# Where the attention visits fire: kept apart, and barred in front of four of fourteen products, with two weight sums moved

## The chip, the cores and the metric

The kernel runs on one core of one Trainium2 chip. The metric is the device time of one execution in microseconds, as the median of several runs. A profiled execution gives the trace from which durations, waits and the chain of waits are read. "us" are microseconds.

## The reference

Two stages that follow one another: an attention whose softmax is replaced by a squared relu, for 8 batches of 12 heads with 448 tokens and head size 64, and a two-layer network with a squared relu on the 3584 resulting tokens.

```python
scores = scale * np.matmul(q, k.transpose(0, 1, 3, 2))
attn = np.maximum(scores, 0.0) ** 2 / S
x = np.matmul(attn, v)                # heads side by side: 3584 x 768
r = np.maximum(x @ w_in, 0.0)         # w_in 768 x 2048
out = (r * r) @ w_out                 # w_out 2048 x 768
```

Inputs and output are in fp32; the kernel computes in fp16 with fp32 sums in PSUM.

## The kernel before

**The work and its stages.** Attention is cut into 24 units (8 batches of 3; four heads a unit) of 7 tiles each, 168 tiles in all. A tile's way: `score` (L246) has TensorE write the scores to one of two PSUM slots (pool `s_p`, L71), then has ACT take their relu into an `at` tile (L258); a DVE multiplication squares it in place (`square`, L371). When the seven tiles of a unit are squared, `av_unit` (L303) runs 28 matmuls into a slot (L319), and ACT copies the result to `xt` (L325). Two tiles are scored per **visit** (`visit`, L373). A visit is named here by its first tile: visit 88 scores tiles 88 and 89. In a visit the first tile is scored, then an AV unit runs if the last tile of a unit was scored in an earlier visit, then the second tile is scored. A visit in which a unit begins also calls `prefetch` (L329): two DMA transposes on SP for the unit two further on, a load of its v and the loads of q and k for a later unit on POOL.

The network is computed for pairs of batches. For the first pair the hidden layer is computed directly (`h_group`, L414, 16 groups a batch). From batch 2 on it goes by a fast scheme with 7 instead of 8 block products (`h_period`, L471): each batch has two periods (`i0` 0 and 4), and each period two sets s of such products, 14 in all, numbered 0 to 13 in the order of the table `order` (L528). A product is six matmuls of 128x224. Some products start a fresh PSUM bank; others add into the bank that an earlier one left, once ACT has copied it (`copy`, L488) or DVE has added from it (`plus`, L493). In that table a row reads: set, block product, which bank of the set, fresh or not, what follows.

```python
(0, 1, 0, True, lambda: copy(0, 0, "m1", "a")),       # product 0
(1, 1, 0, True, lambda: copy(1, 0, "m1", "b")),       # product 1
(0, 6, 0, False, lambda: copy(0, 0, "u2", "c")),      # product 3
(1, 6, 0, False, lambda: copy(1, 0, "u2", "d")),      # product 4
(0, 5, 1, True, lambda: copy(0, 1, "m5", "a")),       # product 6
(0, 7, 0, False, lambda: plus(0, 0, "m5", True, True)),  # product 7
(1, 7, 0, False, lambda: copy(1, 0, "u3", "b")),      # product 8
(0, 4, 0, False, lambda: relu21(0)),                  # product 10
(1, 4, 0, False, lambda: relu21(1)),                  # product 11
```

The second layer (the w_out stage of each pair, `o_groups`, L608) takes pairs of 128-token rows through seven products of eight matmuls (128x384), in the order 1, 2, 6, 5, 7, 4, 3 of their names; the first product of the next pair of rows, or at the end of the stage products of the next h period, run between products 7 and 4 of the pair. Its sums of rows are DVE additions (`sums`, L596, L606), its results go out through ACT (L635, L683) and DVE (L640) to `osb` and by SP to DRAM.

**The order.** `steps` is one list of TensorE matmuls with a planned cost each: 0.1892 in h groups, 0.096 in h periods, 0.1625 in w_out. Their running sum is the planner's clock, which leaves the visits' own time out. `events` is a list of due times on that clock: visits, prefetches, DVE sums. The loop at the end (L906) walks the steps; in front of a step that is marked as an edge it fires all events whose time has come. In an h period the first matmul of every product is an edge (L565), in w_out the first matmul of every product (an edge of the kind 2, product 4, looks 1.6 ahead for one event). [...] the place at which an event fires decides behind which instructions of ACT and DVE its own stand.

The visits of a pair of batches are spread evenly (L861 to L864) from one bound to the next, 6.5 before the end of the first batch's h periods: due times are 2.19 apart while the attention of batches 2 and 3 is done (visits 42 to 82), 3.27 for batches 4 and 5, 2.83 for batches 6 and 7. Sums of x for a pair's first batch (`sums_x`, L453) are due in the last 6 units of the w_out stage before it. Six of the eight sums of w_in (`sums_w1`, L166, one DVE operation of 128x1536 each) fire in batch 1's h groups, two in the first w_out stage (L854); these two make w_in's last block, which block product 7 reads from batch 2 on.

Of the kernel before, what the change touches and what calls it, by code (L numbers as in the profile page):

```python
# [17 lines left out]
def kernel(  # L18
# [147 lines left out]
    def sums_w1(i):  # L166


        op, c = divmod(i, 2)
        now_ve(0.9)  # L170
        lo, hi = slice(0, NM // 2), slice(NM // 2, NM)
        a11, a12, a21, a22 = (w1[c][:, lo], w1[c][:, hi], w1[c + 2][:, lo],
                              w1[c + 2][:, hi])
        if op < 3:
            wsum[op, c] = late["ws"].tile(
                [P, NM // 2, 512], FP16, name=f"ws{op}{c}", tag=f"ws{op}{c}")
        if op == 0:
            nc.vector.tensor_add(wsum[0, c], a21, a22)
        elif op == 1:
            nc.vector.tensor_sub(wsum[1, c], wsum[0, c], a11)  # L180
        elif op == 2:
            nc.vector.tensor_sub(wsum[2, c], a12, wsum[1, c])
        else:
            nc.vector.tensor_sub(a21, a11, a21)
# [144 lines left out]
    def prefetch(m):  # L329
        if m >= NUN:  # L330
            return
        dma_transpose(m)
        if m > NPE:
            load_v(m)
        if m + 2 < NUN:
            load_qk(m + 2)
# [10 lines left out]
    def flush(rest=True):  # L347
        for d in (due, due_g) if rest else (due,):
            while d:
                put(d)  # L350
# [11 lines left out]
    def now_ve(cost, lag=0.25):  # L362
        at_ve[0] = max(at_ve[0], at_pe[0] + lag) + cost
# [5 lines left out]
    def square(at, lag=0.0):  # L369
        due.append((at_pe[0] + lag, 0.54,  # L370
                    lambda: nc.vector.tensor_mul(at, at, at), 0))  # L371

    def visit(tiles, turn=None, lag=2, most=3):  # L373
        now[0] += 1
        for t in tiles:
            if t % J == 0 and t >= NPE * J:
                prefetch(t // J + 2)
        if big:
            for t in tiles[:1]:
                score(t)  # L380
            av_unit()
            for t in tiles[1:]:
                score(t)
            at_pe[0] += 0.19 + 0.19 * len(tiles)
            for i, t in enumerate(tiles):
                square(ats[t], 0.6 + 0.85 * i)
            return
        for t in tiles:
            score(t, 2)
        if turn is not None:  # L390
            pe_transpose(turn)
        flush()
        av_some(lag, most)
        for t in tiles:
            square(ats[t])
        flush()
# [12 lines left out]
    def g_of(b):  # L409
        if b // 2 not in gts:  # L410
            gts[b // 2] = g_p.tile([P, NF, 2 * S], FP16, name="g", tag="g")
        return gts[b // 2]
# [58 lines left out]
    def h_period(b, i0, extra):  # L471

        z = (b % 2) * S
        XY = [[None, None], [None, None]]
        keep: dict = {}

        def gs(s, hi, right=None):
            f = i0 + 2 * s + (8 if hi else 0)
            c = (slice(z, z + S) if right is None
                 else slice(z + Q, z + S) if right else slice(z, z + Q))  # L480
            return g_of(b)[:, f:f + 2, c]

        def acc(s, y):
            return XY[s][y][:, 0:S].rearrange("p (r c) -> p r c", r=2)

        def copy(s, y, nm, tag):
            t = late["m"].tile([P, S], FP32, name=nm, tag=tag)
            nc.scalar.activation(out=t, in_=XY[s][y][:, 0:S], func=AF.Copy)  # L488
            keep[s, nm] = t.rearrange("p (r c) -> p r c", r=2)

        def plus(s, y, nm, hi, right):
            now_ve(0.54)
            nc.vector.tensor_add(gs(s, hi, right), acc(s, y), keep[s, nm])  # L493

        def rest(g, relu, lag):

            t = at_pe[0] + lag
            due_g.append((t, 0.32 if relu is g else 0.2, lambda: nc.vector.tensor_scalar(  # L498
                out=relu, in0=relu, scalar1=0.0, scalar2=None, op0=ALU.max), b))
            due_g.append((t, 0.54, lambda: nc.vector.tensor_mul(g, g, g), b))  # L500

        def relu21(s):
            nc.scalar.activation(out=gs(s, True, False), in_=acc(s, 0), func=AF.Relu)  # L503
            rest(gs(s, True), gs(s, True, True), 0.8)

        def c12(s):
            plus(s, 1, "u2", False, True)
            g = gs(s, False)
            rest(g, g, 0.0)

        def left(k, f, m):

            c, n = f // 4, slice((f % 4) * P, (f % 4 + 1) * P)
            if k in (1, 2):
                return w1[c][:, m + NH * (k - 1), n]
            if k in (4, 7):
                return w1[c + 2][:, m + (NH if k == 4 else 0), n]
            return wsum[{5: 0, 6: 1, 3: 2}[k], c][:, m, n]

        def right(k, m):  # L520
            if k in (1, 2):
                return xts[b][:, m + NH * (k - 1), 0:Q]
            if k in (3, 7):
                return xts[b][:, m + (NH if k == 3 else 0), Q:S]
            return xsum[b, {5: 0, 6: 1, 4: 3}[k]][:, m]


        order = (  # L528
            (0, 1, 0, True, lambda: copy(0, 0, "m1", "a")),
            (1, 1, 0, True, lambda: copy(1, 0, "m1", "b")),  # L530
            (0, 2, 1, True, lambda: plus(0, 1, "m1", False, False)),
            (0, 6, 0, False, lambda: copy(0, 0, "u2", "c")),
            (1, 6, 0, False, lambda: copy(1, 0, "u2", "d")),
            (1, 2, 1, True, lambda: plus(1, 1, "m1", False, False)),
            (0, 5, 1, True, lambda: copy(0, 1, "m5", "a")),
            (0, 7, 0, False, lambda: plus(0, 0, "m5", True, True)),
            (1, 7, 0, False, lambda: copy(1, 0, "u3", "b")),
            (1, 5, 1, True, lambda: plus(1, 1, "u3", True, True)),
            (0, 4, 0, False, lambda: relu21(0)),
            (1, 4, 0, False, lambda: relu21(1)),  # L540
            (0, 3, 1, False, lambda: c12(0)),
            (1, 3, 1, False, lambda: c12(1)))

        FREE = {2: 0.6, 5: 0.6, 7: 0.1, 9: 0.6, 12: 0.6, 13: 1.0, 16: 0.6}

        def step(p, r, m):
            s, k, y, fresh, end = order[p]

            def run():
                if fresh and r == 0 and m == 0 and k != 5:  # L550
                    XY[s][y] = mm_tile(s)
                nc.tensor.matmul(  # L552
                    XY[s][y][:, r * Q:(r + 1) * Q],
                    lhsT=left(k, i0 + 2 * s + r, m), rhs=right(k, m),
                    start=(fresh and r == 0 and m == 0), stop=(m == NH - 1),
                    skip_group_check=not (fresh and r == 0))
                if r == 1 and m == NH - 1:
                    end()
                    for fn in extra.get(p, ()):
                        fn()  # L560
                    nx = min(n for n in FREE if n > p)
                    fill(at_pe[0] + (nx - p) * 0.576 + 0.25 + FREE[nx])
            return run

        return [(0.096, step(p, r, m), r == 0 and m == 0)  # L565
                for p in range(14) for r in range(2) for m in range(NH)]

    def store(row, osb, c, eng, eng2=None):
# [258 lines left out]
    T_H = NF * T_G  # L827
# [4 lines left out]
    events = []  # L832
# [18 lines left out]
    for i in range(6):  # L851
        events.append((T_H + (8 + i) * T_G, lambda i=i: sums_w1(i)))
    for i in range(2):
        events.append((2 * T_H + 3 + 3 * i, lambda i=i: sums_w1(6 + i)))  # L854
    for m in (6, 7):
        events.append((T_H + (1 + 3 * (m - 6)) * T_G, lambda m=m: prefetch(m)))
    at0 = T_H + 8 * T_G
    for pr in range(1, B // 2):
        t0 = 2 * NB0 * pr
        end = begin[pr] + T_S - 6.5  # L860
        gap = (end - at0) / 21  # L861
        for i in range(21):
            ts = [t0 + 2 * i, t0 + 2 * i + 1]
            events.append((at0 + i * gap, lambda ts=ts: visit(ts)))  # L864
        at0 = end
        for i in range(4):
            events.append((begin[pr] - 6 + i, lambda b=2 * pr, i=i: sums_x(b, i)))
    events.append((at0 + 0.3, lambda: visit([])))

    def pre(pr, i):  # L870
        def run():
# [29 lines left out]
                steps += periods[b, i0]  # L901
        steps += outs[pr][0]

    clock = 0.0
    ev = deque(sorted(events, key=lambda e: e[0]))
    for cost, fn, edge in steps:  # L906
        fired = 0
        while ev and edge and ev[0][0] <= clock + (1.6 if edge == 2 and not fired else 1e-3):
            ev.popleft()[1]()
            fired += 1  # L910
        if fn is not None:
            at_pe[0] += cost
            fn()
        clock += cost
# [31 lines left out]
```

## Time and profile before

| | |
|---|---|
| Time, median of three runs | 377.74 us (377.57 to 377.84) |
| The profiled execution | 377.92 us, span 376.1 us |
| Granted TensorE clock | 0.999 |
| h periods of batches 2 and 3 | 123.75 to 167.1 us |
| w_out stage of the second pair, with the first products of batch 4 | 167.1 to 217.1 us |
| h periods of batches 4 and 5 | 217.1 to 260.5 us |
| w_out stage of the third pair | 260.5 to 297.7 us |

In lines of the profile, PE is TensorE's matmuls, PEld its weight loads, DVE VectorE, ACT ScalarE, POOL GpSimd, SPq the queue that issues DMAs on SyncE. A line of the timeline has the start, the time from the first start to the last end, engine, line and operation, "out<-in" with the names of the tiles, the shape, and how many instructions are merged in it. In brackets stands how long the engine had been idle and what ended that. The first of two overlapping records is not shortened, so the distance between starts says more than the lengths. L254 are scores, L319 AV units, L552 products of h periods, L733 products of w_out.

### The profile page before, as it was taken

Reading aid. Unit: us, or ns where it says so; the run is one execution under the profiler, and the core shown is the slowest. Engines: PE = TensorE matmul, PEld = TensorE weight load, DVE = VectorE, ACT = ScalarE, POOL = GpSimd, SP = SyncE. Lnnn points to the kernel's source line nnn. Section 1 sums busy time; section 2 is a strip of 40 time slices with the busy share of each in tenths; the row PEclk is TensorE's granted clock in tenths of the full one; section 3 lists DMA queues with packets and bytes.
Section 4 is the critical chain, followed back from the end, with each engine's and each line's share of the span. In section 5 each row is a group of like instructions: output and inputs, shape, how many; then the busy total and the mean of one; then the engine's idle time right before and its main releaser. Section 6 shows DMA issues by size and latency. Waiting matters only on the chain.

```text
span 376.1 us, 8798 instructions
## 1 busy us (share of the span) xinstructions
PE 363.3 (97%) x3600; PEld 231.1 (61%) x3600; DVE 280.4 (75%) x518; ACT 247.6 (66%) x370; POOL 107.2 (29%) x128
## 2 busy tenths in 40 slices
PE   7899999999999999999999999999999999999994
PEld 3554444454555778875555578877455588985663
DVE  1886677997767699797775758978966788995542
ACT  2997894786777797776665678887666785531220
POOL 8545431837432354413043144050000000000001
PEclk9999999999999999999999999999999999999999
DMA  8999999999999999959699999692232300002333
GB/s 115 199 204 205 204 204 149 132 140 129 203 138 175 157 129 122 91 81 75 115 117 129 195 153 86 83 103 53 49 86 65 83 23 2 2 0 65 95 95 84
DMA packets 121159, 42.64 MB, mean 113 GB/s; under 512 B 100832, under 2 KB 117760, under 8 KB 121120
## 3 DMA queue, kind: packets, MB, share of 16 engines
q0 software_dynamic: 82912, 23.01, 62.6%
q1 hardware_dynamic: 38048, 18.98, 26.4%
q8 instruction: 28, 0.46, 0.5%
q10 hardware_dynamic: 160, 0.10, 0.1%
q14 instruction: 11, 0.09, 0.1%
HBM read 45.61 MB, written 11.01 MB: 151 GB/s over the span
## 4 chain that ended last, share of the span: by engine, by line
PE 80%; DVE 9%; ACT 6%; issue 2%; DMA 1%; POOLq 0%; POOL 0%; ACTq 0%; DVEq 0%
PE mm L733 31%; PE mm L552 22%; PE mm L422 9%; PE slot L254 9%; PE slot L319 7%; ACT at L258 5%; DVE at L371 3%; DVE g L493 1%; DVE g L500 1%; DMA q<-in_q_dram 1%; DVE s L606 1%; PE slot L225 1%; DVE osb L640 1%; DVE g L498 1%; ACT m L488 1%
## 5 line engine op out<-in xcount | busy, mean ns | idle before, releaser
L258 ACT ACTIVATE at<-slot 128x896 f16<-128x896 f32 x168 | 146.0, 920 | 32.6 <-PE slot L254 32.5
L371 DVE TENSOR_TENSOR at<-at 128x896 f16<-128x896 f16 x168 | 99.9, 618 | 19.3 <-ACT at L258 18.8
L108 POOL DMA_DIRECT2D qs<-in_q_dram x36 | 35.5, 987 | 117.7 <-DMA qT<-qs 110.0
L733 PEld LDWEIGHTS <-s 128*128 128x128 f16 x440 | 41.6, 98 | 32.4 <-issue 3.9
L254 PE MATMUL slot<-qT,kT 64*64 64x448 f16 x756 | 57.9, 360 | 2.3 <-ACT at L258 1.6
L552 PEld LDWEIGHTS <-w 128*128 128x128 f16 x576 | 54.4, 98 | 5.9 <-issue 5.4
L552 PE MATMUL mm<-xt,w 128*128 128x224 f16 x432 | 48.6, 259 | 0.0
L733 PEld LDWEIGHTS <-g 128*128 128x128 f16 x336 | 31.5, 98 | 24.0 <-issue 5.0
L552 PEld LDWEIGHTS <-ws 128*128 128x128 f16 x432 | 40.2, 98 | 6.7 <-issue 6.7
L733 PE MATMUL mm<-b,g 128*128 128x384 f16 x224 | 40.7, 326 | 0.0
L733 PE MATMUL mm<-b,s 128*128 128x384 f16 x216 | 39.6, 326 | 0.3 <-DVE s L606 0.2
L422 PE MATMUL mm<-xt,w 128*128 128x448 f16 x192 | 39.8, 354 | 0.0
L733 PE MATMUL mm<-t,s 128*128 128x384 f16 x224 | 39.5, 326 | 0.0
L254 PEld LDWEIGHTS <-kT 64*64 64x64 f16 x756 | 19.9, 104 | 30.4 <-issue 25.5
L108 POOL DMA_DIRECT2D ks<-in_k_dram x36 | 35.0, 975 | 11.5 <-DMA b<-in_moe_w_out_dram 5.8
L640 DVE SCALAR_TENSOR_TENSOR osb<-mm,u 128x384 f32<-128x384 f32 (+1 forms) x30 | 16.2, 542 | 27.0 <-ACT u L635 19.3
L635 ACT ACTIVATE u<-mm 128x384 f32<-128x384 f32 x28 | 13.7, 491 | 33.2 <-PE mm L733 31.8
L573 POOL DMA_DIRECT2D out_dram<-osb x2 | 1.1, 564 | 120.7 <-DVE osb L640 120.7
L552 PE MATMUL mm<-x,ws 128*128 128x224 f16 x288 | 34.4, 259 | 0.9 <-ACT m L488 0.9
L319 PE MATMUL slot<-at,vt 64*64 64x448 f16 x588 | 32.2, 350 | 0.8 <-DVE at L371 0.7
L500 DVE TENSOR_TENSOR g<-g 128x896 f16<-128x896 f16 x48 | 29.7, 619 | 1.1 <-ACT g L503 0.2
L493 DVE TENSOR_TENSOR g<-mm,m 128x448 f16<-128x448 f32 x36 | 22.0, 619 | 9.4 <-ACT m L488 4.1
(69 smaller groups left out, 395.6 us busy)
## 6 DMA issues: line engine op xcount, KB each, us to landing
out_dram<-osb SPq DMA_DIRECT2D x52, 192.0 KB, 3.3
vt<-in_v_dram POOLq DMA_DIRECT2D x24, 224.0 KB, 6.9
qs<-in_q_dram POOLq DMA_DIRECT2D x36, 112.0 KB, 5.3
ks<-in_k_dram POOLq DMA_DIRECT2D x36, 112.0 KB, 5.6
w<-in_moe_w_in_dram POOLq DMA_DIRECT2D x8, 384.0 KB, 11.7
b<-in_moe_w_out_dram POOLq DMA_DIRECT2D x4, 768.0 KB, 17.1
q<-in_q_dram POOLq DMA_DIRECT2D x6, 224.0 KB, 8.1
k<-in_k_dram POOLq DMA_DIRECT2D x6, 224.0 KB, 8.5
```

Of the source, the lines that this page charges most:

```text
L108: nc.gpsimd.dma_start(out=t[:, :, hh, :], in_=heads(src, n)[:, hh].rearrange("p (j d) -> p j d", d=D))
L254: nc.tensor.matmul(ps[c, hh, 0:S], lhsT=kT[r, j, c], rhs=qT[r, :, c], start=True, stop=True)
L258: nc.scalar.activation(out=at, in_=ps[:, :, 0:S], func=AF.Relu, scale=SK)
L319: nc.tensor.matmul(ps[64 * hh:64 * hh + 64, hp, 0:S], lhsT=vt[r, hh, j * D:(j + 1) * D], rhs=at[r, hh, :], start=(j == 0), stop=(j == J - 1))
L371: lambda: nc.vector.tensor_mul(at, at, at), 0))
L422: nc.tensor.matmul(cell[0][:, 0:S], lhsT=w1[f // 4][:, m, (f % 4) * P:(f % 4 + 1) * P], rhs=xts[b][:, m, :], start=(m == 0), stop=(m == NM ...
L493: nc.vector.tensor_add(gs(s, hi, right), acc(s, y), keep[s, nm])
L500: due_g.append((t, 0.54, lambda: nc.vector.tensor_mul(g, g, g), b))
L552: nc.tensor.matmul(XY[s][y][:, r * Q:(r + 1) * Q], lhsT=left(k, i0 + 2 * s + r, m), rhs=right(k, m), start=(fresh and r == 0 and m == 0), ...
L635: nc.scalar.activation(out=t, in_=X[0][:, 0:HALF], func=AF.Copy, scale=CO)
L640: nc.vector.scalar_tensor_tensor(out=osb[row][:, c], in0=acc[0][:, 0:cc.stop - cc.start], scalar=CO, in1=keep[nm][:, cc], op0=ALU.mult, op ...
L733: nc.tensor.matmul(acc[0][:, 0:HALF], lhsT=left()[:, f], rhs=right[:, f], start=(fresh and f == 0), stop=(f == KH - 1), skip_group_check=n ...
```

## The change

- In an h period the first matmul of products 0, 1, 6 and 8 is no longer an edge: no event of any kind fires in front of them.
- Visits of batches 2 to 7 carry a third entry. Such an event fires only if the clock is at least 1.5 past the last one that fired; otherwise the loop stops there for this step, and the events behind it in the list wait as well.
- The two sums of w_in in the first w_out stage are due 6 and 14 after its begin, where they were due 3 and 6 after it.

```diff
-        return [(0.096, step(p, r, m), r == 0 and m == 0)
+        return [(0.096, step(p, r, m), r == 0 and m == 0 and p not in (0, 1, 6, 8))
                 for p in range(14) for r in range(2) for m in range(NH)]
...
-        events.append((2 * T_H + 3 + 3 * i, lambda i=i: sums_w1(6 + i)))
+        events.append((2 * T_H + 6 + 8 * i, lambda i=i: sums_w1(6 + i)))
...
-            events.append((at0 + i * gap, lambda ts=ts: visit(ts)))
+            events.append((at0 + i * gap, lambda ts=ts: visit(ts), True))
...
-    events.append((at0 + 0.3, lambda: visit([])))
+    events.append((at0 + 0.3, lambda: visit([]), True))
...
-    clock = 0.0
+    clock, last = 0.0, 0.0
...
         while ev and edge and ev[0][0] <= clock + (1.6 if edge == 2 and not fired else 1e-3):
+            if len(ev[0]) == 3:
+                if clock < last + 1.5:
+                    break
+                last = clock
             ev.popleft()[1]()
             fired += 1
```

## The prediction

> **What bounds the kernel now.** I read the page first (busy shares, chain of waits), then the timeline of TensorE over the h and w_out stages, then ACT's and DVE's timelines round each gap.
>
> ```profile
> PE 363.3 (97%) x3600; PEld 231.1 (61%) x3600; DVE 280.4 (75%) x518; ACT 247.6 (66%) x370; POOL 107.2 (29%) x128
> ...
> PE 80%; DVE 9%; ACT 6%; issue 2%; DMA 1%; POOLq 0%; POOL 0%; ACTq 0%; DVEq 0%
> ```
>
> TensorE carries 80% of the chain, ACT and DVE 15%: what can be won is where TensorE stands still for one of those two. A record of a matmul is longer than the distance to the next, so I measure by starts. In the h periods a product of six matmuls starts 0.576 us after the one before it; a visit of two tiles in between adds 0.60, and one that also holds an AV unit adds 1.92 (28 matmuls, 1.32). Whatever goes beyond that is a stall. TensorE in the first period of batch 3:
>
> ```profile
> 146.24 0.57 PE L254 MATMUL slot<-qT,kT 64*64 64x448 f16 x8
> 146.75 1.32 PE L552 MATMUL mm<-xt,w 128*128 128x224 f16 x12
> 147.91 0.74 PE L552 MATMUL mm<-x,ws 128*128 128x224 f16 x6
> 149.06 0.73 PE L552 MATMUL mm<-x,ws 128*128 128x224 f16 x6 [0.41 <-ACT m L488]
> ...
> 152.54 0.74 PE L552 MATMUL mm<-x,ws 128*128 128x224 f16 x6
> 153.61 1.31 PE L552 MATMUL mm<-x,w 128*128 128x224 f16 x12 [0.33 <-DVE g L493]
> ```
>
> 147.91 to 149.06 is 1.15 for a product of 0.576: a stall of 0.576. Product 4 adds into the bank that product 1 left, and must wait for ACT's copy of it. ACT at that time:
>
> ```profile
> 146.41 0.54 ACT L488 ACTIVATE m<-mm 128x448 f32<-128x448 f32 x1 [1.03 <-PE mm L552]
> 146.85 1.72 ACT L258 ACTIVATE at<-slot 128x896 f16<-128x896 f32 x2
> 148.44 0.56 ACT L488 ACTIVATE m<-mm 128x448 f32<-128x448 f32 x1
> ```
>
> The visit stood in front of product 1, so its two relus of scores (starts 0.80 apart) lie ahead of product 1's copy. At 153.61 the same goes by way of DVE: the visit in front of product 6 delays the copy of m5, the addition after product 7 waits for it, product 10 for the addition.
>
> The w_out stages have another sort of stall, between visits that stand close together:
>
> ```profile
> 90.76 0.56 DVE L640 SCALAR_TENSOR_TENSOR osb<-mm,u 128x384 f32<-128x384 f32 x1 [0.90 <-ACT u L635]
> 91.24 1.15 DVE L371 TENSOR_TENSOR at<-at 128x896 f16<-128x896 f16 x2
> 92.44 0.38 PE L319 MATMUL slot<-at,vt 64*64 64x448 f16 x4 [0.15 <-DVE at L371]
> ...
> 120.01 0.38 PE L254 MATMUL slot<-qT,kT 64*64 64x448 f16 x4 [0.26 <-ACT at L258]
> 120.82 0.38 PE L254 MATMUL slot<-qT,kT 64*64 64x448 f16 x4 [0.43 <-ACT at L258]
> ```
>
> First an AV unit waits for squares of tiles scored one product earlier; then scores wait for the two slots in PSUM. From 80 us to the end all stalls over 0.025 us sum to 6.75 us, the most that any order of this work could save there.
>
> [...] the copy starts at 148.44, 1.59 after the two relus ahead of it began. [...] here 97% busy hides those 6.75 us. [...] The trace has records of 0.92 and 0.55 and, back to back, starts 0.80 and 0.43 apart; I use the last.
>
> **The change, part by part.** An event fires at the first allowed step at which the planner's clock has reached its due time, so both orders can be worked out by hand from the step costs and due times. For the order before, each visit so placed shows up in the trace at its product.
>
> *Products 0, 1, 6 and 8 barred.* Removed, with the stall read at each: visit 88 (named by its first tile) from product 1 to 2 of batch 3 (149.06: 0.576); 90 from 6 to 7 (153.61: 0.492); 120 from 1 to 2 of batch 4 (219.19: 0.408); 122 from 6 to 7 (223.74: 0.492); 128 from 8 to 9 of its second period (235.92: 0.407); 136 from 0 to 2 in batch 5's second period (251.63: 0.407). These are all the stalls of over 0.1 us in the h periods but the 0.220 of the last AV unit, which stays. Sum **2.78**. Do the new places cost as much? In front of 2, the copies of products 0 and 1 are ahead of the relus; the next copy needed is product 3's, delayed to 2.05 after the visit's start and wanted by product 7 at 3.4. In front of 7, product 8's copy ends 2.6 after it and product 11 starts at 2.8. The trace has visits in front of 2 (124.42), 7 (303.18), 9 (142.19) and 12 (154.85) without a stall over 0.046. I take nothing.
>
> *Visits kept 1.5 apart.* On the planner's clock visits 54/56, 56/58, 60/62, 64/66 and 146/148 are 1.30 apart and 72/74 are 0.58. The second of each pair carries a stall: 1.024 (92.95), 0.109 (94.96), 0.114 (101.50), 0.110 (108.05), 0.552 (272.59) and 0.955 (121.14). They become 2.60 apart or, 72/74, 1.73, so the waiting work has at least 1.15 more, over any of these. Sum **2.86**.
>
> *What this pushes together.* Blocked visits hold back all events behind them. In the first w_out stage visits end up 2.60 apart and the surplus runs into batch 2: eight visits (72 to 86, in front of 2, 5, 9, 12 twice) where there were six. In that stretch:
>
> ```profile
> 123.75:134.98 11.23, 11.23 (x139) 8.60 (x138) 8.10 (x14) 9.54 (x15) 2.36 (x4) 1.00 1.24 167
> 134.98:145.58 10.60, 10.60 (x131) 9.06 (x130) 9.82 (x20) 9.18 (x15) 8.79 (x10) 1.00 1.61 136
> ```
>
> The columns after the length are PE, weight loads, DVE, ACT and POOL. ACT is busy 18.7 of 21.8 us; four more relus (3.2) make 21.9 of 23.0, as the two visits bring 1.2 us of TensorE work from elsewhere. DVE has 17.9; four more squares at 0.535 make 20.1. Both still fit, ACT barely. Walking ACT's queue through the two periods with these spacings, I find one wait: visit 78 holds an AV unit, its second score needs the slot of its first, whose relu then ends about 0.17 late. Bounds: nothing, or a stall of the kind above (mean 0.46) after four of the eight visits, 1.9. I take **0.4**: the 0.17 and half a stall.
>
> *The sums of w_in.* Two DVE additions of 0.95 move from 40.23 and 42.83 on the clock to 42.83 and 51.93; their results are first read by product 7 of batch 2's two periods, clock 67.7 and 75.7. Count and engine stay; nothing queued behind them on DVE is needed within 0.95. Zero. The sums of x for batch 2 are held back by at most 3.8; the last is read by product 10, 4.6 later. Zero.
>
> *DMAs moved along.* Every seventh tile's visit issues two transposes on SP and, on POOL, a load of v and four of q and k. They move up to 4.9 later, but what reads them is the visit seven further on, which moves too. The shortest distance, visit 70 to 84, is 15.3 of clock plus seven visits (4.2) and two AV units (2.6), about 22 us; transposes land 2.9 to 10.5 us after issue. On SP the order of stores and transposes stays as it is; POOL's waits are for its own buffers. Zero.
>
> Sum: 2.78 + 2.86 - 0.4 = **5.25**. The profiled execution has a span of 376.1, so 370.9 there; it was timed at 377.92, against a median of 377.74, so 377.74 - 5.25 = **372.5**.
>
> **Rivals.** *Crowding in batch 2 or 3 (17%).* The 1.9 above applies in place of 0.4: 374.0; with DVE's squares of g pushed into batch 3, where it was idle only some 2.3 of 21.5 us, up to 374.6. For it: ACT at 95%. Against: visits in front of 6, 10 and 13 at 128 to 134 us were as dense and cost nothing.
>
> *Only the h stalls go (10%).* DVE, not the spacing, holds the w_out stalls and they come back elsewhere: 377.74 - 2.78 + 0.4 = 375.4. For it: DVE is in the chain throughout 262 to 272. Against: spacing undoes the wait at 120.82 by construction.
>
> *Slower (4%).* Score slots in batch 2: with two slots and ACT behind, each of the eight visits waits as visit 74 did, 0.955 each, 7.6 in all: 377.74 - 5.25 + 7.6 = 380.1. It decides from the sixth visit that waits in full. Against: 1.73 of clock plus 0.6 is more than the 1.6 that two relus take.
>
> *It does nothing that can be told (3%)*: stalls are made good later, at the DVE-bound end of a stage: 377.7.
>
> **How the numbers follow.** My own case has 66%, from 371.8 (no cost at all, and some of the other 1.1 us of stalls gone too) to 373.5. Reaching to 374.6 takes in the crowding rival and leaves out the others, about 2 in 10. Runs of before lie within 0.27 us; 0.2% is 0.75 us, about what can be told from no change. Faster 0.93, same 0.03, slower 0.04.
>
> **What would show it.** Right: no PE wait on L488 or L493 in batches 3 to 5 over 0.1 us; the six w_out stalls gone; batch 2's two periods about 1.6 us longer (two visits and the 0.4). Wrong: new waits on "ACT m", "ACT u" or "ACT at" at 125 to 150 us beyond 1 us in all, or the DVE waits before L319 still there.

## The result: a quarter of the gain that was forecast

| | before | changed |
|---|---|---|
| Median, six runs each | 377.71 us (377.57 to 378.11) | 376.38 us (375.29 to 376.92) |
| Ratio to before, 95% interval | | 0.9959 (0.994 to 0.9978) |
| Span of the profiled execution | 376.1 us | 375.1 us |
| Granted TensorE clock there | 0.999 | 0.994 |
| All stalls from 80 us on, by starts (slowed matmuls included) | 6.75 us | 5.95 us |

The change makes the kernel faster by 1.3 us; 5.25 was forecast, in a range whose slow end was 374.6 us. The six runs of the changed kernel fall in two groups: three at 376.88 to 376.92 with a granted clock of 0.993 or 0.994 (the profiled one among them), three at 375.29 to 375.89 with 0.998 or 0.999. Why is part of the finding.

**The profile after.** The page's rows that were shown of before (line numbers behind L562 are two higher here):

```profile
PE 363.1 (97%) x3600; PEld 230.9 (62%) x3600; DVE 279.8 (75%) x518; ACT 247.7 (66%) x370; POOL 107.4 (29%) x128
...
PEclk9999999999999999999899999999999999999999
...
PE 83%; DVE 8%; ACT 4%; issue 2%; DMA 1%; POOL 0%; POOLq 0%; DVEq 0%; ACTq 0%
```

ACT and DVE have fallen from 15% to 12% of the chain. New is an 8 in the row of the clock, in the slice of 178 to 188 us.

The places that the prediction walked through look as forecast. TensorE and ACT in the first period of batch 3, where visit 88 had cost 0.576:

```profile
144.87 0.57 PE L254 MATMUL slot<-qT,kT 64*64 64x448 f16 x8
145.37 0.75 PE L552 MATMUL mm<-xt,w 128*128 128x224 f16 x6
145.96 1.31 PE L552 MATMUL mm<-x,ws 128*128 128x224 f16 x12
147.11 0.74 PE L552 MATMUL mm<-xt,w 128*128 128x224 f16 x6
```

```profile
144.46 1.06 ACT L488 ACTIVATE m<-mm 128x448 f32<-128x448 f32 x2 [0.23 <-PE mm L552]
145.42 1.72 ACT L258 ACTIVATE at<-slot 128x896 f16<-128x896 f32 x2
```

Both copies (144.46) now stand ahead of the two relus, and products 3 and 4 (145.96, twelve matmuls in one piece) run through. The AV unit of the first w_out stage, which had waited a microsecond for squares, starts at 91.30 right behind its scores:

```profile
91.09 0.38 PE L254 MATMUL slot<-qT,kT 64*64 64x448 f16 x4
91.30 1.49 PE L319 MATMUL slot<-at,vt 64*64 64x448 f16 x28
```

All twelve stalls that the prediction took off (5.65 us) are gone. What came in their place is in the second w_out stage:

```profile
177.74 0.57 PE L254 MATMUL slot<-qT,kT 64*64 64x448 f16 x8
178.24 1.47 PE L735 MATMUL mm<-b,g 128*128 128x384 f16 x8
181.87 4.29 PE L735 MATMUL mm<-t,s 128*128 128x384 f16 x16 [2.15 <-DVE s L608]
186.08 0.50 PE L254 MATMUL slot<-qT,kT 64*64 64x448 f16 x4
```

From 178.24 to 181.87 pass 3.63 us for eight matmuls of 0.163 each: a stall of 2.32, in which TensorE waits for the row sums of the second pair of row blocks. Then sixteen matmuls take 4.2 us where 2.6 are usual. The windows view of TensorE for 3.41 us of that (length, PE busy, clock, DMA share, GB/s) has the clock at half:

```profile
182.96:186.37 3.41, 3.41 (x15) 0.50 1.08 156
```

DVE's timeline shows what stands ahead of the row sums (174.69 is an output addition, L608 the row sums):

```profile
174.69 0.55 DVE L642 SCALAR_TENSOR_TENSOR osb<-mm,u 128x384 f32<-128x384 f32 x1
175.16 0.62 DVE L500 TENSOR_TENSOR g<-g 128x896 f16<-128x896 f16 x1
175.69 0.39 DVE L498 TENSOR_SCALAR g<-g 128x896 f16<-128x896 f16 x1
176.12 0.63 DVE L500 TENSOR_TENSOR g<-g 128x896 f16<-128x896 f16 x1
...
179.31 0.39 DVE L498 TENSOR_SCALAR g<-g 128x896 f16<-128x896 f16 x1
179.74 0.62 DVE L500 TENSOR_TENSOR g<-g 128x896 f16<-128x896 f16 x1
180.40 0.69 DVE L608 TENSOR_TENSOR s<-g 128x1024 f16<-128x1024 f16 x1
181.12 0.69 DVE L608 TENSOR_TENSOR s<-s,g 128x1024 f16<-128x1024 f16 x1
```

Eleven operations that finish g, the hidden activations (relu L498, square L500), stand there in a row, 5.2 us. They are work of batch 3's h periods. `rest` (L495) does not issue them but puts them into the queue `due_g`; `fill` (L357) issues them when the planner sees room on DVE; and before a second pair of row blocks is summed, `ahead` (L622) calls `flush_g(2 * B)`, which issues all that is left, since the sums read g. Of the eleven, `fill` issues the first two behind product 7 and `flush_g` the other nine. Before the change there were four, one by `fill` and three by `flush_g`:

```profile
177.82 0.55 DVE L640 SCALAR_TENSOR_TENSOR osb<-mm,u 128x384 f32<-128x384 f32 x1
178.29 0.38 DVE L498 TENSOR_SCALAR g<-g 128x896 f16<-128x896 f16 x1
178.70 0.63 DVE L500 TENSOR_TENSOR g<-g 128x896 f16<-128x896 f16 x1
179.24 0.39 DVE L498 TENSOR_SCALAR g<-g 128x896 f16<-128x896 f16 x1
179.66 0.63 DVE L500 TENSOR_TENSOR g<-g 128x896 f16<-128x896 f16 x1
180.32 0.69 DVE L606 TENSOR_TENSOR s<-g 128x1024 f16<-128x1024 f16 x1
181.05 0.69 DVE L606 TENSOR_TENSOR s<-s,g 128x1024 f16<-128x1024 f16 x1
```

The product that reads these sums started at 182.57 then, without a stall:

```profile
181.26 1.47 PE L733 MATMUL mm<-b,g 128*128 128x384 f16 x8
182.57 2.76 PE L733 MATMUL mm<-t,s 128*128 128x384 f16 x16
```

**The theory**, then: with the visits in their new places, two more of them in batch 2, more of g is left undone, the put-out in the second w_out stage grows from 4 to 11 operations, and the stall that this makes, 2.32 us, is what halves TensorE's clock in some runs (0.50 for 3.41 us in the profiled one). **Rivals**: the spacing of visits alone does it by crowding batch 2; the half clock comes by itself and has nothing to do with the stall; crowding itself, not the put-out, eats the gain.

### The profile page after: what moved, and what is told of

It reads as the page before. It is cut to its first block, busy times and chain, and to the rows that moved or that the text cites. A ratio compares the mean times of both kernels' runs of the same rounds, so it can differ in the third digit from the quotient of the medians.

```text
span 375.1 us, 8794 instructions
## 1 busy us (share of the span) xinstructions
PE 363.1 (97%) x3600; PEld 230.9 (62%) x3600; DVE 279.8 (75%) x518; ACT 247.7 (66%) x370; POOL 107.4 (29%) x128
## 4 chain that ended last, share of the span: by engine, by line
PE 83%; DVE 8%; ACT 4%; issue 2%; DMA 1%; POOL 0%; POOLq 0%; DVEq 0%; ACTq 0%
PE mm L735 30%; PE mm L552 26%; PE mm L422 9%; PE slot L254 9%; PE slot L319 7%; ACT at L258 4%; DVE at L371 2%; DVE g L500 2%; DVE s L608 1%; DMA k<-in_k_dram 1%; DVE g L498 1%; PE slot L225 1%; DVE osb L642 1%; DVE xt L285 1%; PE mm L225 0%
## 5 line engine op out<-in xcount | busy, mean ns | idle before, releaser
L735 PE MATMUL mm<-t,s 128*128 128x384 f16 x224 | 40.9, 335 | 2.2 <-DVE s L608 2.2
L319 PE MATMUL slot<-at,vt 64*64 64x448 f16 x588 | 31.9, 350 | 0.2 <-DVE at L371 0.2
L500 DVE TENSOR_TENSOR g<-g 128x896 f16<-128x896 f16 x48 | 29.9, 622 | 1.3
```

The source lines that it names most:

```text
L319: nc.tensor.matmul(ps[64 * hh:64 * hh + 64, hp, 0:S], lhsT=vt[r, hh, j * D:(j + 1) * D], rhs=at[r, hh, :], start=(j == 0), stop=(j == J - 1))
L735: nc.tensor.matmul(acc[0][:, 0:HALF], lhsT=left()[:, f], rhs=right[:, f], start=(fresh and f == 0), stop=(f == KH - 1), skip_group_check=n ...
```

## The experiments

"The put-out" is the row of finishing operations in the second w_out stage. The kernel before, run beside the experiments, had medians of 377.74 to 377.81 us.

**1. The bar alone.** The first line of the diff, nothing else.

```diff
-        return [(0.096, step(p, r, m), r == 0 and m == 0)
+        return [(0.096, step(p, r, m), r == 0 and m == 0 and p not in (0, 1, 6, 8))
```

> Only the four products are barred; visits may stand as close as before, and the two sums of w_in are where they were. Theory (each stall taken from TensorE also takes time from DVE, whose left-over squares of g are all put out at once in the second w_out stage): the six h stalls (2.78 us) go, visits 72 and 74 are 1.30 apart in place of 0.58 and lose about 0.7 of 0.955, and the put-out holds 7 operations in place of 4, so the second pair of row blocks waits about 0.4 us for its sums: 374.6 us. Rival (crowding of batch 2 by the spacing alone makes the new stall): no stall there, 374.2 us. In both the w_out stalls of 1.02 and 0.55 us stay.

Measured: 374.82 us, ratio 0.9917 (0.9901 to 0.9934). No h stall of over 0.1 us is left but the last AV unit's 0.22; visit 74 waits 0.22 in place of 0.955; the put-out holds 7 operations and the stall behind it is 0.19. A wait of 0.23 for ACT is new in the third w_out stage, at visit 160. So the bar alone gives 2.9 us, more than the whole change. The stall at the put-out was smaller than expected but there, without any spacing; the rival's 374.2 was missed as well.

**2. The spacing alone.** The whole change with the old marks of edges and the old times of the two sums.

```diff
-        return [(0.096, step(p, r, m), r == 0 and m == 0 and p not in (0, 1, 6, 8))
+        return [(0.096, step(p, r, m), r == 0 and m == 0)
...
-        events.append((2 * T_H + 6 + 8 * i, lambda i=i: sums_w1(6 + i)))
+        events.append((2 * T_H + 3 + 3 * i, lambda i=i: sums_w1(6 + i)))
```

> Only the visits are kept 1.5 apart; no product is barred, the sums of w_in are where they were. Theory: w_out stalls of 2.86 us go, the six h stalls of 2.78 stay, visit 72 falls in front of product 0 and costs a new 0.4; the put-out of squares holds 9 operations, stall about 1.3 us, with the AV unit and slot waits of the changed kernel (0.6): 377.2 us. Rival (spacing alone makes the whole stall of 2.3 us and the half clock): stall 2.3 us and 378 to 379 us.

Measured: 377.75 us over twelve runs, ratio 1.0001 (0.9992 to 1.0009): no change. The w_out stalls (2.86) are gone; in their place stand 1.15 at the put-out of nine operations, 0.47 at an AV unit, 0.36 in batch 2, and 0.98 where visit 72 falls in front of product 0, which was expected at 0.4:

```profile
120.98 1.32 PE L552 MATMUL mm<-xt,w 128*128 128x224 f16 x12
123.12 0.73 PE L552 MATMUL mm<-x,ws 128*128 128x224 f16 x6 [0.82 <-ACT m L488]
```

These sum to 2.96, which eats the gain to a tenth. Their stall of 1.15 brought no half clock in the profiled run (mean clock 0.998), and eleven of the twelve runs lie within 377.61 to 378.04.

**3. Bar and sums, no spacing.**

```diff
+        return [(0.096, step(p, r, m), r == 0 and m == 0 and p not in (0, 1, 6, 8))
...
+        events.append((2 * T_H + 6 + 8 * i, lambda i=i: sums_w1(6 + i)))
```

> The change without the spacing: products barred and the two sums of w_in later. Both theories: as with the bar alone, within 0.3 us (374.6 us), since the sums delay nothing that is on the path. If the sums matter, the AV unit's stall of 1.02 us in the first w_out stage would shrink here and not with the bar alone.

Measured: 374.62 us, ratio 0.9915 (0.99 to 0.993), and stall by stall the same as the bar alone, the AV unit's 1.02 included. The moved sums of w_in are worth nothing that can be told. Spacing added on top of this kernel makes it 1.8 us slower.

**4. The change, with g finished earlier.** Up to two operations of the queue are issued in every AV unit, whether or not the planner sees room for them.

```diff
         flush(rest=False)
+        for _ in range(min(2, len(due_g))):
+            put(due_g)
         at_pe[0] += 1.33
```

> The whole change, and in each AV unit up to two of the left-over operations on g are put out on DVE, so that 4 are left for the put-out in the second w_out stage where the change has 11. Theory (the put-out is the stall, and the stall brings the half clock): stall of 2.3 us gone, granted clock 0.998 or more in every run, 373.0 us. Rival 1 (the half clock comes by itself, from load): clock 0.993 in about half of the runs, 373 to 374.6 us. Rival 2 (crowding of batch 2 itself costs the gain): no better than 375.5 us.

Measured: 372.98 us (372.94 to 373.18), ratio 0.9872 (0.9857 to 0.9887). The put-out holds four operations again and TensorE (line numbers four higher than in the kernel before) runs on:

```profile
178.29 1.47 PE L737 MATMUL mm<-b,g 128*128 128x384 f16 x8
179.60 2.76 PE L737 MATMUL mm<-t,s 128*128 128x384 f16 x16
182.29 0.38 PE L254 MATMUL slot<-qT,kT 64*64 64x448 f16 x4
```

The profiled run has no half clock, and the times lie within 0.24 us. The mean clock is 0.996 to 1.0: two of the four runs are below the 0.998 that was expected, but the kernel before has 0.996 to 1.0 too. All stalls from 80 us on sum to 2.00 where they were 6.75; the difference, 4.75, fits the gain in time, 4.76. Crowding in batch 2 as such costs little: the rivals that need it fall.

**5. A longer stall at the same place.** The change, and ten small memsets of a tile that nothing reads any more, behind the put-out.

```diff
                     flush_g(2 * B)
+                    if len(groups) == 4:
+                        while more[0]:
+                            more[0] -= 1
+                            nc.vector.memset(zeros, 0.0)
```

> The whole change, and behind the eleven put-out operations ten small DVE memsets of a tile that is no longer read (some 2.0 to 2.4 us), which only lengthen the stall in the second w_out stage. Theory[...]: stall 4.3 to 4.7 us, and[...] the half clock in every run, not in half of them: 379 to 379.5 us, mean clock 0.99 to 0.994 in all. Rival (the half clock comes by itself): still in only some runs, 377.6 in the others.

Measured: 380.57 us (380.35 to 380.76), ratio 1.0075 (1.006 to 1.009). The memsets took 3.4 us, not 2.0 to 2.4, so the stall is 5.60 and the time over what was expected:

```profile
178.18 1.47 PE L740 MATMUL mm<-b,g 128*128 128x384 f16 x8
185.09 4.89 PE L740 MATMUL mm<-t,s 128*128 128x384 f16 x16 [5.44 <-DVE s L609]
```

The clock is 0.988 to 0.992 in all four runs, where the change had it low in three of six; the page's row of the clock falls to 6 in that slice. With a stall of 0.2 (experiments 1 and 3) or none (4) it is 0.996 or more. A longer stall at the same place, and nothing else, brings the low clock in every run, which is what the theory asks for. What decides whether a stall of 2.32 brings it was not controlled, so that "half of the runs" is a count of six and not a rate.

**6. Three operations in place of two.**

```diff
-        for _ in range(min(2, len(due_g))):
+        for _ in range(min(3, len(due_g))):
```

> The whole change, and up to three (not two) left-over operations put out in each AV unit. Theory: nothing more to win, since with two the stall was gone already: 373.0 us within 0.3. A third operation may also come too early and hold up a square: up to 373.5.

Measured: 372.94 us (372.9 to 373.06), ratio 0.9874 (0.9859 to 0.9888). As expected, nothing more.

**7. The kernel before, with g finished earlier.** The diff of experiment 4 on the kernel before.

> The kernel before with only the putting out of two left-over operations in each AV unit. Theory (before the change the put-out in the second w_out stage was not on the path): no gain, 377.7 us within 0.4. Rival (the early putting out is a gain of its own, which hid the change's true worth in the run before): 376.5 us or less.

Measured: 377.33 us over twelve runs (377.06 to 377.87), ratio 0.999 (0.9981 to 0.9998). A gain of 0.4 to 0.5, at the edge of what was expected, and not the 1.3 of the rival: the AV unit's stall of 0.55 in the third w_out stage shrinks to 0.17, the other stalls stay. The early finishing is worth 3.4 us on the changed kernel and under 0.5 on the old one.

**8. The bar, with g finished earlier.** The diff of experiments 1 and 4.

> Products barred and two left-over operations put out in each AV unit; visits not kept apart, sums of w_in where they were. Theory: the 0.19 us of stall that the bar alone left in the second w_out stage goes: 374.6 us, so that the spacing, once the put-out is off the path, is worth the rest to 373.0: 1.6 us. Rival (the bar did all of it and spacing is worth nothing): 373.2 us.

Measured: 374.36 us (373.97 to 375.94), ratio 0.9919 (0.9896 to 0.9941). The stall of 0.19 is gone; one of 0.16 is new in batch 2. So with the put-out off the path the spacing (and the sums) are worth 374.36 - 372.98 = 1.4 us; with it on the path they cost 1.6 on top of the bar. One of the four runs, at 375.94 with a clock of 0.995, stands apart. That looks like the half clock, in a kernel whose profiled run has no stall at the put-out; it was not profiled, so that other causes of a half clock are not excluded.

**9. Sums of x earlier**, on top of experiment 6.

```diff
-            events.append((begin[pr] - 6 + i, lambda b=2 * pr, i=i: sums_x(b, i)))
+            events.append((begin[pr] - 9 + i, lambda b=2 * pr, i=i: sums_x(b, i)))
```

> The whole change with up to three operations put out in each AV unit, and the sums of x for a pair's first batch due 3 units of the planner's clock earlier. In the last two w_out stages that have h periods behind them a sum of x (0.42 us on DVE) stands between the squares and the row sum that product 7 or 4 waits for (stalls of 0.36 and 0.23 us). Theory: they go, 372.4 us. Rival (the sums only meet other work on DVE): within 0.2 us of 372.9.

Measured: 372.89 us, ratio 0.9868 (0.9851 to 0.9884). A miss: of the two stalls the 0.23 is gone, the 0.36 stays, and a new one of 0.23 stands in batch 3.

## Why the prediction was wrong

**The sum of what is removed was right.** 2.78 in the h periods and 2.86 in w_out were read from starts, and each of the twelve stalls is gone in the changed kernel. With the put-out kept at four operations (experiment 4) the kernel runs in 372.98 us; 372.5 was forecast.

**The step that failed is "What this pushes together", in the sentence "Both still fit, ACT barely".** It compared the time that DVE's work needs in batch 2 with the time that there is. DVE even had more room than that: in batch 2's two periods (windows view; PE, weight loads, DVE, ACT, POOL) it worked 17.9 of 23.2 us, where 20.1 was forecast.

```profile
120.38:143.62 23.24, 23.24 (x284) 17.93 (x282) 17.86 (x34) 21.23 (x33) 9.69 (x12) 1.00 1.31 133
```

In experiment 4 the same stretch has the same length, with four more operations on DVE and 19.32 us of work:

```profile
120.42:143.66 23.24, 23.24 (x284) 17.92 (x282) 19.32 (x38) 21.22 (x33) 10.78 (x12) 1.00 1.16 135
```

So the finishing of g was not crowded out by a lack of time. The planner held it back while DVE stood idle for over 5 us, since `fill` issues such an operation only if, by the planner's own costs, it ends within a window behind a product, and squares of tiles go first. The planner sees no stalls, so what it leaves can be counted from the program alone, without the chip: at the end of batch 2 the queue holds 7 operations before the change, 7 with the bar alone, 11 with the spacing alone and 11 with both; at the end of batch 3 it holds 10, 13, 15 and 16; in the put-out, where the traces show the same counts, 4, 7, 9 and 11. It is the new order of the visits that fills the queue, then, and not, as experiment 1 had supposed, the time that a removed stall takes from DVE.

The prediction knew of the work ("squares of g pushed into batch 3", in its crowding rival) but did not follow it to `flush_g(2 * B)`, where the rest is forced out, and to the row sums that stand behind it: at that place it put nothing, and 2.32 us were measured there. Its bound on the unknown cost, 1.9 us, came from stalls of another kind and was too small. Its signs missed it too: those of being right came true (batch 2's periods grew by 1.41 for about 1.6), and those of being wrong looked for new waits at 125 to 150 us or for the old ones before L319, while the stall stood at 180 us before a product of w_out. By count of operations the stall there is 0 for 4, 0.19 for 7, 1.15 for 9 and 2.32 for 11: once the margin is used up, some 0.5 us for each operation, about what one takes on DVE (eleven took 5.2 us). The 0.8 us of margin before the change can be read off too: the second row sum ended at 181.74, and its product began at 182.57.

**A second cost, unforeseen, came on top.** The half clock in the profiled run: sixteen matmuls in 4.2 us in place of 2.6, some 1.6 lost with the visit behind them, which answers to the 1.0 to 1.6 between the two groups of runs. The clock was 0.50 for 3.41 us here, and over the 6.83 us from 182.61 on in experiment 5. Here it fell at 182.96, when TensorE had been at work again for 1.09 us behind the stall of 2.32; in experiment 5 it was already at half for the last 2.48 us of the stall. What sets these lengths and moments the runs do not show.

**The smaller terms.** Slot wait of visit 78: 0.17 forecast, 0.16 measured. Batch 2's periods: "about 1.6 us longer" forecast, 1.41 measured. Not foreseen: 0.47 at the AV unit of visit 70, which the spacing moved to 1.88 on the planner's clock behind visit 68 where 2.60 had lain between them, so that it waits for squares as visit 56 had done; and 0.23 in the third w_out stage, where the bar took visit 160 from in front of a product that waits for ACT, so that "I take nothing" was wrong there. The three sum to 0.86 where 0.4 was taken. The sums of w_in at zero (experiment 3) and the DMAs at zero (no wait of a score for a transpose in the trace) were right.

**The rivals.** "Crowding in batch 2 or 3" named the right work but the wrong place and price. "Only the h stalls go" has the number nearest to the time measured, 375.4, and a stall did come back on DVE; but it was not one of those in w_out that DVE had held, since in experiment 4 all of these stay gone. Its number is near by luck.

| step | forecast | measured |
|---|---|---|
| six h stalls | -2.78 | -2.78 |
| six w_out stalls | -2.86 | -2.86 |
| new waits by crowding | +0.4 | +0.16 + 0.47 |
| a new wait for ACT by the bar | 0 | +0.23 |
| the put-out before the row sums | 0 | +2.32 |
| the half clock | none | +1.6 in three of six runs |

Of 5.65 removed, 2.32 + 0.86 are left off in the runs without the half clock: 2.5, against 377.71 - 375.46 = 2.25 in the middle one of them.

## What to carry to other kernels

Where software holds work back in a queue of its own, look up where that queue is forced to empty, count what will be in it there, and ask what stands behind it: that the engine has idle time does not mean that the work is done in it. If the planner goes by its own costs, as here, the count can be had before any run. When a change has two parts, run each alone and both together: here one alone (2.9 us) beats both (1.3), and both with the queue emptied early (4.8) beat either.

## What the runs showed that was not expected

A TensorE stall of 2.32 us was followed by 3.41 us at half clock (0.50) in the profiled run, and by a low mean clock (0.993 or 0.994) in three of six runs. With a stall of 5.60 the half clock lasted 6.83 us in the profiled run, the first 2.48 of them still within the stall, and the mean clock was low (0.988 to 0.992) in four of four. A stall of 1.15 brought none in its profiled run (mean clock 0.998). On DVE ten memsets of 128x224 words in a row took 3.47 us, 0.35 each, where a single one at the start of the kernel has a record of 0.245.
